# Another hand-written order for the loading phase of an attention and gated-FFN kernel on Trainium2

## Chip, core and metric

The kernel runs on one NeuronCore of a Trainium2 chip. PE is the matrix engine (its weight loads are PEld), DVE the vector engine, ACT the scalar engine, POOL is GpSimd, SP the engine that issues DMAs. Each engine works through its own queue in order; engines meet at semaphores. The metric is device time per execution in microseconds (us), as the median of several runs. The change is judged against 0.5%, about 1.13 us.

## What is computed

```python
# x (8, 8, 512, 64), state (8, 8, 32, 64): batch, head, row, depth
a  = softmax(x @ state^T / 8)        # each of 512 rows over 32 states
a2 = softmax(state @ x^T / 8)        # each of 32 states over 512 rows
y  = concatenate([a @ state, a2 @ x], axis=rows)   # per batch 512 + 32 rows
t  = heads of y side by side          # 8*544 = 4352 rows of 512
out = (sigmoid(t @ w_gate) * (t @ w_val)) @ w_out  # w: 512x1536, 1536x512
```

Both softmaxes come from one exponential of the scores. The kernel uses bfloat16 operands and float32 accumulation; the sigmoid is written as (tanh(z/2)+1)/2, its half folded into the last copy.

## The kernel before, in words

For one batch b the work runs as follows. `load_x` brings x in float32 (tile xf), `cast_x` makes bfloat16 of it (xb), two of eight heads at a time. x is transposed to xT, for batches 0 and 1 on PE into PSUM with a copy out (`xT_mm`, `xT_cp`, L101-L119), for the others by DMA transposes on SP's queue (`at_xT_dma`, L121). The state is loaded (`load_s`, `load_sb`), transposed on PE (`sT_mm`) and copied into sTc (`sT_cp`) or, zero-padded by head parity, into sTz (`sT_pad`, `pad`). `S_mm` makes the scores and `S_exp` their exponentials E on ACT. From E come Eb in bfloat16 (`at_Eb`, POOL), row sums and normalised weights ab (`n_sum`, `n_mul`, DVE), and aT, ab transposed (`aT_mm` and `aT_cp`, or `aT_dma`). Sums over rows for the second softmax are folded on POOL (`p_tok`, `p_fold`) or made on PE, and `sr_mm`, `sr_fin` give the 32 state rows.

The first product is regrouped: state @ w_gate and state @ w_val come first (`sw_visit`, `sw_wide`, L271-L302, into PSUM; `sw_cp`, L304, copies them to the tile SW), and `gv_mm(b, f, place)` multiplies SW by aT: two PSUM banks, gate and value, for the f-th 128 of 1536 columns, four matmuls of 512 columns. `gv_th` (tanh, ACT) reads the gate bank, `gv_glu` (DVE) the value bank, and glu is the left side of the second product, `out_mm(b, k)`: four matmuls each, three k for each quarter c of a batch's rows, then a copy on ACT and a store through SP.

PSUM has eight banks: two in the pool GV, one each in OU and AT, four in SWP. A call's `place` names the pool it takes a bank from; the bank is free once its last reader has run.

The order is written out by hand, one call after another, under `tc.manual_schedule()`: what is written first stands first in its engine's queue. L424-L673 are the prologue: batches 0 and 1 in full up to the product, the weights' loads, and batch 2 up to its aT. From L675 a loop over b = 2 to 8 pairs the second product of batch b-1 with the first product of b and prepares b+1; b = 8 stands for the state rows of all batches. The loop is the same before and after.

These parts of the prologue matter here:

- `warm(n, place)` (L381) issues n matmuls of 128 columns on the constant tile `ones`, whose results nobody reads. They keep PE busy ahead of its first real work.
- Weights are loaded with a cast on POOL's queue (`load_w(w, lo, n)` for columns lo to lo+n of w_gate (w=0) or w_val (w=1); `load_wo(q)` for a third of w_out). POOL also casts, folds and pads, and its DMAs stand in its queue between these.
- `pre` is a tile whose first column is filled by a first Exp (L438).
- `gate(landed)` (L80) is a POOL copy of one column of a tile, so that POOL's queue waits until that tile has landed. L594 puts one on batch 2's xT right ahead of load_wo(1); load_wo(2) follows it in the queue.
- For batch 2, cast_x(2) (POOL and DVE, L571 and L582) leads to at_xT_dma(2) (L590), S_mm(2) (L608, L610) and then n_sums, n_muls and aT_dma(2).

Of the kernel before, what the change touches and what calls it, by code (L numbers as in the profile page):

```python
# [16 lines left out]
def kernel(  # L17
# [70 lines left out]
    def cast_x(b, cp, lo, n):  # L88
        if b not in xbs:
            xbs[b] = xp.tile((128, 4, H, D), BF, name="xb")  # L90
        cp(xbs[b].rearrange("p c h d -> p h c d")[:, lo:lo + n], xfs[b][:, lo:lo + n])  # L91
# [289 lines left out]
    def warm(n, place):  # L381

        ps = place[0].tile((128, 512), FP, name="warm", tag=place[1])
        for _ in range(n):
            nc.tensor.matmul(ps[:, :128], ones[:, 0], ones[:, 0], start=True, stop=True)
# [39 lines left out]
    load_x(0, nc.sync, 4)
    load_x(1, nc.sync, 4)
    make_identity(nc, ident)
    for e in range(2):
# [1 line left out]
        nc.vector.memset(ones[:, e, 64 - e * 64:128 - e * 64], 0.0)  # L430
    nc.vector.memset(sTz, 0.0)
# [5 lines left out]
    pre = wp.tile((128, 2), FP, name="pre")
    nc.scalar.activation(pre[:, 0:1], ones[:, 0, 0:1], AF.Exp)  # L438

    cast_x(0, pool, 0, 2)  # L440
    load_w(1, 256, 256)
    load_w(0, 256, 256)
    load_sb(1)
    cast_s(0, vec)
    cast_x(0, pool, 4, 2)
    warm(20, SWP)
    load_w(0, 1024, 512)
    warm(16, OU)
    xT_mm(0, 0, OU)
    sT_mm(0, SWP)  # L450
    xT_cp(0, 0, vec)
    warm(20, OU)
    cast_x(0, act, 2, 2)
    cast_x(0, vec, 6, 2)
    xT_mm(0, 1, SWP)
    sT_pad(0, 0, vec)
    sT_pad(0, 1, act)
    S_mm(0, 0, SWP, (0,))
    xT_cp(0, 1, vec)
    xT_mm(0, 2, OU)  # L460
    cast_x(1, vec, 2, 2)
    cast_x(1, pool, 0, 2)
    xT_mm(0, 3, GV)
    load_w(1, 1024, 512)
    xT_cp(0, 2, act)
    cast_x(1, pool, 6, 2)
    xT_cp(0, 3, vec)
    cast_x(1, vec, 4, 2)
    load_w(0, 0, 256)
    load_sb(3)  # L470
    S_mm(0, 0, AT, (1,))
    S_exp(0, 0)
    S_mm(0, 1, AT, (0,))
    xT_mm2(1, 0, OU)
    S_mm(0, 1, OU, (1,))
    S_exp(0, 1)
    warm(12, AT)
    xT_cp2(1, 0, act)
    n_sum(0, 0)
    xT_mm2(1, 1, SWP)  # L480
    S_mm(1, 0, GV)
    n_sum(0, 1)
    xT_cp2(1, 1, vec)
    S_mm(1, 1, SWP)
    S_exp(1, 0)
    at_Eb(0)
    sw_visit(0, 256, 256)
    n_mul(0, 0, nc.vector)
    n_mul(0, 1, nc.vector)
    S_exp(1, 1)  # L490
    sT_mm(1, GV)
    sw_cp(0, 256, 2, 1, act)
    p_tok(1)
    n_sums(1)
    sw_cp(0, 256, 2, 0, act)
    aT_mm(0, GV)
    sT_cp(1, act)
    aT_cp(0, 0, act)
    sr_mm(0, AT)
    sw_visit(1, 256, 256)  # L500
    sw_visit(0, 1024, 512, 0)
    aT_cp(0, 1, vec)
    n_muls(1, nc.vector)
    load_sb(2)
    gv_mm(0, 3, GV)
    sw_cp(1, 256, 2, 0, act)
    sw_cp(1, 256, 2, 1, act)
    gv_th(0, 3)
    load_w(1, 0, 256)
    aT_mm(1, OU)  # L510
    sw_cp(0, 1024, 0, 1, act)
    sw_visit(1, 1024, 512, 0)
    sw_cp(0, 1024, 0, 0, vec)
    gv_glu(0, 3)
# [4 lines left out]
    sw_visit(1, 1024, 512, 1)
    sw_cp(0, 1024, 1, 1, vec)  # L520
    gv_mm(0, 11, GV)
    aT_cp(1, None, vec)
    sw_cp(1, 1024, 1, 0, act)
    gv_mm(0, 2, SWP)
# [8 lines left out]
    load_x(2, nc.gpsimd)
    gv_mm(0, 9, SWP)
    gv_glu(0, 11)
    gv_mm(1, 8, GV)
    gv_th(0, 9)
# [7 lines left out]
    gv_glu(1, 8)
    sw_cp(1, 0, 2, 1, act)
    gv_mm(0, 8, GV)
    sT_mm(2, AT)
    sw_cp(1, 0, 2, 0, act)
    sw_visit(0, 512, 512, 0)  # L550
    sw_cp(0, 0, 2, 0, vec)
# [6 lines left out]
    gv_mm(1, 11, GV)
    load_wo(0)
    sw_cp(0, 512, 0, 0, act)  # L560
    sw_cp(0, 512, 0, 1, vec)
    gv_th(1, 11)
    gv_mm(0, 0, SWP)
    gv_glu(1, 11)
    gv_mm(1, 9, GV)
    sw_cp(1, 512, 0, 1, act)
    at_Eb(1)
    sw_cp(1, 512, 0, 0, act)
    gv_th(1, 9)
# [9 lines left out]
    sr_mm(1, AT)
    gv_glu(0, 1)  # L580
    gate(xfs[0][:, 7, 0, 0:1])
    cast_x(2, pool, 0, 4)  # L582
    sw_visit(0, 512, 512, 1)
# [15 lines left out]
    sr_fin(1)
    gv_mm(0, 6, SWP)  # L600
    gv_mm(0, 7, GV)
    gv_mm(0, 4, SWP)
    gv_th(0, 6)
    gv_th(0, 7)
    out_mm(0, 1, OU)
# [1 line left out]
    gv_th(0, 4)
    S_mm(2, 1, SWP)  # L608
    gv_mm(1, 4, SWP)
    S_mm(2, 0, GV)  # L610
    gv_glu(0, 4)
    gv_glu(0, 7)
# [3 lines left out]
    gv_mm(1, 6, GV)
    gv_th(1, 4)
    gv_th(1, 6)
    out_mm(0, 0, AT)
    gv_glu(1, 6)  # L620
    gv_mm(1, 7, GV)
    gv_glu(1, 4)
# [4 lines left out]
    n_sums(2)
    load_x(3, nc.gpsimd)
    out_mm(0, 3)
    n_add(2)  # L630
# [1 line left out]
    n_muls(2, nc.vector)
    out_mm(0, 9)
    at_Eb(2)
    aT_dma(2)
# [1 line left out]
    out_mm(0, 4)
    gv_th(1, 3)
    gv_glu(1, 3)
    out_mm(0, 5)  # L640
    out_mm(0, 11)
    gv_mm(1, 1, GV)
    gv_th(1, 1)
    sw_wide(2, 0)
    out_mm(0, 6, GV)
# [4 lines left out]
    sw_cp(2, 0, 1, 1, act)  # L650
    sw_cp(2, 0, 2, 1, act)
    sw_cp(2, 0, 0, 0, vec)
    out_mm(0, 8)
    cast_x(3, pool, 0, 4)
    sw_cp(2, 0, 2, 0, act)
    sw_wide(2, 1)
    cast_x(3, act, 4, 4)
    sw_cp(2, 1, 1, 0, act)
    sw_cp(2, 1, 0, 0, act)
# [1 line left out]
    at_xT_dma(3)
    sw_cp(2, 1, 1, 1, vec)
    out_mm(0, 10)
    sw_cp(2, 1, 2, 1, vec)
    gv_mm(1, 10, SWP)
    sw_cp(2, 1, 0, 1, vec)
# [88 lines left out]
```

## Time and profile before

| what | value |
|---|---|
| time, median of 3 runs | 226.27 us (226.02 to 227.07) |
| span of the profiled execution, first to last instruction | 225.4 us |
| difference of the two | 0.87 us |
| first real PE work (a transpose of x) | 4.97 us |
| first gate/value matmuls, gv_mm(0, 3) | 16.20 us |
| wo thirds landed | 32.56, 44.09, 47.38 us |
| batch 2's xT: transposes issued, last landed | 29.95, 37.67 us |
| x(3) landed | 50.98 us |
| first sw_wide of the loop | 57.56 us |

Times inside the profile count from its first instruction. The timeline's rows read: start, duration, engine, line, operation, tile written <- tiles read, shape, number of instructions merged, and in brackets the idle time of the engine ahead of the row with what ended it. A row of several PE matmuls lasts from the start of its first to the end of its last, and the end of one lies well behind the start of the next.

### The profile page before, as it was taken

How to read it: one execution, taken by the hardware profiler on the slowest of the kernel's cores; microseconds unless marked ns; L12 is line 12 of the kernel's file. 1: busy time of each engine (PE TensorE's matmuls, PEld its weight loads, DVE VectorE, ACT ScalarE, POOL GpSimd, SP SyncE). 2: the span in 40 equal slices, each digit the busy share in tenths (PEclk: the TensorE clock that was granted, in tenths of full speed). 3: DMA queues.
4: the chain of work that ended last, by engine and by line, in shares of the span. 5: the costliest groups of instructions: out<-in, count | busy, mean ns of one | idle time of the engine just before them, and what ended most of it. 6: DMA issues, size and time to landing. Idle time of an engine off the chain costs nothing.

```text
span 225.4 us, 4817 instructions
## 1 busy us (share of the span) xinstructions
PE 216.1 (96%) x1843; PEld 110.5 (49%) x1843; DVE 132.2 (59%) x228; ACT 128.7 (57%) x242; POOL 77.6 (34%) x164
## 2 busy tenths in 40 slices
PE   7689999899999999999999999999999999999994
PEld 6654444334444444444444444444445444466744
DVE  3799997647658554855585638574766434422301
ACT  3468885339576566757574666656755444433311
POOL 4999832481027502660068005900370000000001
PEclk9999999999999999999999999999999999999999
DMA  6999992995496245614671441236112111111113
GB/s 208 276 204 193 287 157 48 138 261 167 92 292 223 47 93 165 210 35 86 153 245 26 86 126 47 69 70 143 47 61 81 48 47 49 72 69 49 47 33 108
DMA packets 38503, 27.38 MB, mean 121 GB/s; under 512 B 21104, under 2 KB 33776, under 8 KB 38480
## 3 DMA queue, kind: packets, MB, share of 16 engines
q1 hardware_dynamic: 31344, 19.74, 31.2%
q0 software_dynamic: 6848, 7.14, 17.1%
q8 instruction: 14, 0.23, 0.4%
q10 hardware_dynamic: 288, 0.20, 0.4%
q14 instruction: 9, 0.07, 0.1%
HBM read 18.35 MB, written 8.91 MB: 121 GB/s over the span
## 4 chain that ended last, share of the span: by engine, by line
PE 74%; DMA 12%; SPq 4%; POOL 4%; ACT 3%; issue 1%; DVE 1%; POOLq 0%
PE outp L351 34%; PE gvp L320 28%; DMA xf<-in_x_dram 6%; PE gvp L323 5%; SPq L124 4%; DMA wo<-in_moe_w_out_dram 4%; PE swp L268 3%; DMA xT<-xb 2%; PE Sp L132 2%; PE outp L371 1%; ACT SW L306 1%; PE srp L245 1%; POOL sTz L420 1%; SPq L74 1%; ACT E L137 1%
## 5 line engine op out<-in xcount | busy, mean ns | idle before, releaser
L335 DVE SCALAR_TENSOR_TENSOR glu<-th,gvp 128x512 bf16<-128x512 f32 (+1 forms) x108 | 70.0, 656 | 75.9 <-ACT th L330 61.8
L351 PE MATMUL outp<-wo,glu 128*128 128x512 bf16 x396 | 98.5, 379 | 1.2 <-DMA wo<-in_moe_w_out_dram 1.2
L320 PE MATMUL gvp<-aT,SW 128*128 128x512 bf16 x384 | 96.5, 379 | 0.0
L330 ACT ACTIVATE th<-gvp 128x512 f32<-128x512 f32 (+1 forms) x108 | 61.5, 574 | 59.2 <-PE gvp L320 47.1
L320 PEld LDWEIGHTS <-SW 128*128 128x128 bf16 x384 | 36.3, 98 | 45.1 <-issue 3.7
L351 PEld LDWEIGHTS <-glu 128*128 128x128 bf16 x396 | 37.4, 98 | 42.3 <-issue 2.2
L306 ACT CAST SW<-swp 128x512 bf16<-128x512 f32 x73 | 40.5, 588 | 3.9 <-PE swp L268 2.5
L143 POOL CAST Eb<-E 128x256 bf16<-128x256 f32 x32 | 12.0, 427 | 63.1 <-ACT E L137 63.1
L355 ACT ACTIVATE res<-outp 128x512 f32<-128x512 f32 x33 | 19.7, 597 | 19.6 <-PE outp L351 19.5
L362 POOL DMA_DIRECT2D out_dram<-res x2 | 1.1, 532 | 52.4 <-ACT res L355 52.4
L306 DVE CAST SW<-swp 128x512 bf16<-128x512 f32 x23 | 15.2, 681 | 0.0
L91 POOL CAST xb<-xf 128x1024 bf16<-128x1024 f32 (+1 forms) x14 | 12.8, 927 | 3.2 <-DMA xf<-in_x_dram 2.6
L137 ACT ACTIVATE E<-Sp 128x512 f32<-128x512 f32 x16 | 9.6, 602 | 3.4 <-PE Sp L132 3.4
L183 POOL COPY F<-G 32x128 f32<-32x128 f32 x28 | 9.9, 353 | 1.3
L204 DVE TENSOR_TENSOR ab<-E,ri 128x512 bf16<-128x512 f32 x12 | 8.7, 735 | 0.0
L268 PE MATMUL swp<-wg,sTc 64*32 64x512 bf16 (+1 forms) x192 | 8.6, 328 | 0.0
L132 PE MATMUL Sp<-sTz,xT 128*128 128x64 bf16 x128 | 7.0, 193 | 1.6 <-DVE xT L119 0.6
L132 PEld LDWEIGHTS <-xT 128*128 128x128 bf16 x128 | 6.0, 98 | 5.1 <-DVE xT L119 0.7
L178 POOL COPY F<-E 64x128 f32<-64x128 f32 x14 | 4.1, 292 | 12.3 <-DVE E L170 11.8
L150 DVE TENSOR_REDUCE rs<-E 128x16 f32<-128x512 f32 x12 | 8.2, 679 | 0.2 <-ACT E L137 0.2
L268 PEld LDWEIGHTS <-sTc 64*32 64x32 bf16 x384 | 4.5, 91 | 7.6 <-issue 5.4
L250 DVE RECIPROCAL r<-srp 128x128 f32<-128x128 f32 x8 | 7.6, 949 | 0.7 <-PE srp L245 0.7
(75 smaller groups left out, 150.3 us busy)
## 6 DMA issues: line engine op xcount, KB each, us to landing
out_dram<-res SPq DMA_DIRECT2D x31, 256.0 KB, 2.6
xf<-in_x_dram SPq DMA_DIRECT2D x4, 1024.0 KB, 6.3
xf<-in_x_dram SPq DMA_DIRECT2D x8, 256.0 KB, 4.5
xf<-in_x_dram POOLq DMA_DIRECT2D x2, 1024.0 KB, 10.1
wo<-in_moe_w_out_dram POOLq DMA_DIRECT2D x3, 512.0 KB, 8.3
wg<-in_moe_w_gate_dram POOLq DMA_DIRECT2D x2, 512.0 KB, 7.4
wv<-in_moe_w_val_dram POOLq DMA_DIRECT2D x2, 512.0 KB, 9.8
wv<-in_moe_w_val_dram POOLq DMA_DIRECT2D x2, 256.0 KB, 5.5
```

The costliest lines, as they stand in the source:

```text
L91: cp(xbs[b].rearrange("p c h d -> p h c d")[:, lo:lo + n], xfs[b][:, lo:lo + n])
L132: nc.tensor.matmul(ps[:, c, :, jj], xTs[b][:, 2 * i + jj, c], sTz[:, b, 2 * i + jj], start=True, stop=True)
L137: nc.scalar.activation(E1s[b][:, :, :, 2 * i:2 * i + 2].rearrange("p c e j n -> p (c e) j n"), held["S", b, i].rearrange("p c e j n -> p ( ...
L143: nc.gpsimd.tensor_copy(Ebs[b][:, c], E1s[b][:, c])
L268: nc.tensor.matmul(pss[e][j * Ns:(j + 1) * Ns, o:o + n], sTc[rows, b, j] if b > 1 else sTz[rows, b, j, e], (wg, wv)[w][rows, j, lo:lo + n] ...
L306: cp(*sw_left.pop((b, lo, w, e)))
L320: nc.tensor.matmul(ps, SWs[b][:, g, w, fs], aTs[b][:, :, g], start=(g == 0), stop=(g == 1))
L323: nc.tensor.matmul(ps, (wg, wv)[w][:, j, fs], XS[:, j], start=(j == 0), stop=(j == 3))
L330: nc.scalar.activation(th, held["gv", b, f][0], AF.Tanh, scale=0.5)
L335: nc.vector.scalar_tensor_tensor(glus[b][:, f], held["th", b, f], 1.0, held["gv", b, f][1], ALU.add, ALU.mult)
L351: nc.tensor.matmul(ops[b, c], glus[b][:, f, c * 128:(c + 1) * 128], wo[:, f], start=(f == 0), stop=(f == NF - 1))
L355: nc.scalar.activation(res, ops[b, c], AF.Copy, scale=0.5)
```

## The change

The calls from L424 to L673 are written in another order, with some other engines and PSUM pools; the loads, matmuls and counts of work are the same but for the warm matmuls (68 in four calls before, 68 in four calls after, with other sizes ahead of the first transposes). All of L424-L673 is replaced by the new list, of which this is the core (leading lines whole up to gv_mm(0, 3)):

```diff
+    load_x(0, nc.sync, 4)
+    load_s(0, nc.scalar)
+    make_identity(nc, ident)
+    load_x(1, nc.sync, 4)
+    nc.vector.memset(sTz, 0.0)
+    for e in range(2):
+        nc.vector.memset(ones[:, e, e * 64:e * 64 + 64], 1.0)
+        nc.vector.memset(ones[:, e, 64 - e * 64:128 - e * 64], 0.0)
+    cast_s(0, pool)
+    warm(20, GV)
+    load_w(0, 256, 256)
+    warm(20, GV)
+    cast_x(0, vec, 0, 2)
+    sT_mm(0, OU)
+    xT_mm(0, 0, GV)
+    load_w(1, 256, 256)
+    sT_pad(0, 1, act)
+    sT_pad(0, 0, vec)
+    xT_cp(0, 0, vec)
+    nc.scalar.activation(pre[:, 0:1], ones[:, 0, 0:1], AF.Exp)
+    warm(16, AT)
+    cast_x(0, pool, 2, 2)
+    cast_x(0, act, 4, 2)
+    cast_x(1, vec, 0, 2)
+    load_w(0, 1024, 512)
+    xT_mm(0, 1, SWP)
+    load_w(1, 1024, 512)
+    cast_x(0, act, 6, 2)
+    load_sb(2)
+    nc.gpsimd.memset(pick, 0.0)
+    xT_mm(0, 2, GV)
+    S_mm(0, 0, SWP, (0,))
+    xT_cp(0, 2, vec)
+    load_sb(1)
+    xT_cp(0, 1, act)
+    xT_mm(0, 3, SWP)
+    cast_x(1, vec, 2, 2)
+    S_mm(0, 0, OU, (1,))
+    S_mm(0, 1, AT, (0,))
+    xT_cp(0, 3, act)
+    S_mm(0, 1, AT, (1,))
+    cast_x(1, pool, 4, 2)
+    S_exp(0, 0)
+    cast_x(1, act, 6, 2)
+    load_w(0, 0, 256)
+    xT_mm2(1, 0, SWP)
+    n_sum(0, 0)
+    xT_mm2(1, 1, OU)
+    S_exp(0, 1)
+    at_Eb(0)
+    xT_cp2(1, 0, vec)
+    warm(12, GV)
+    S_mm(1, 0, GV)
+    xT_cp2(1, 1, act)
+    load_sb(3)
+    n_mul(0, 0, nc.vector)
+    S_mm(1, 1, OU)
+    n_sum(0, 1)
+    n_mul(0, 1, nc.vector)
+    load_w(1, 0, 256)
+    S_exp(1, 0)
+    sw_visit(0, 256, 256)
+    S_exp(1, 1)
+    sw_cp(0, 256, 2, 1, act)
+    sw_visit(1, 256, 256)
+    sr_mm(0, OU)
+    sw_cp(1, 256, 2, 1, act)
+    aT_mm(0, AT)
+    sw_visit(1, 1024, 512, 0)
+    load_w(0, 512, 512)
+    sw_cp(1, 256, 2, 0, act)
+    gate(xfs[0][:, 7, 0, 0:1])
+    n_sums(1)
+    sw_cp(0, 256, 2, 0, act)
+    aT_cp(0, 1, vec)
+    aT_cp(0, 0, act)
+    sw_visit(0, 1024, 512, 0)
+    n_muls(1, nc.vector)
+    gv_mm(0, 3, GV)
+    sw_cp(0, 1024, 0, 1, vec)
+    sw_cp(1, 1024, 0, 0, act)
+    gv_th(0, 3)
+    sw_cp(1, 1024, 0, 1, vec)
+    aT_mm(1, AT)
+    p_tok(1)
+    sw_cp(0, 1024, 0, 0, act)
+    sw_visit(1, 1024, 512, 1)
+    aT_cp(1, None, act)
+    gv_glu(0, 3)
+    sw_visit(0, 1024, 512, 1)
+    sw_cp(0, 1024, 1, 1, act)
...
+    at_Eb(1)
+    sw_cp(0, 1024, 1, 0, act)
+    sr_fin(0)
+    sw_cp(1, 1024, 1, 1, act)
+    gv_mm(0, 2, GV)
+    gv_mm(0, 11, SWP)
+    load_x(2, nc.gpsimd)
+    sw_cp(1, 1024, 1, 0, vec)
...
+    sT_mm(2, GV)
+    sT_mm(1, OU)
+    load_w(1, 512, 512)
...
+    sT_mm(3, AT)
+    sT_cp(2, vec)
...
+    load_wo(0)
...
+    p_fold(1)
...
+    gv_mm(1, 11, GV)
...
+    sT_cp(1, vec)
...
+    cast_x(2, pool, 0, 4)
+    load_wo(1)
...
+    cast_x(2, pool, 4, 4)
...
+    gv_mm(0, 5, SWP)
+    sw_cp(1, 512, 1, 1, vec)
+    sT_cp(3, act)
...
+    at_xT_dma(2)
...
+    out_mm(0, 1, AT)
+    pad(2, 6)
...
+    load_wo(2)
...
+    out_mm(0, 0, OU)
+    S_mm(2, 0, GV)
+    load_x(3, nc.gpsimd)
+    S_mm(2, 1, SWP)
...
+    gv_mm(1, 7, SWP)
+    n_sums(2)
+    n_muls(2, nc.vector)
+    n_add(2)
+    cast_x(3, vec, 4, 4)
+    gv_th(1, 7)
+    out_mm(0, 3)
+    out_mm(0, 2)
+    at_Eb(2)
+    gv_mm(1, 3, GV)
+    gate(xTs[2][:, 0, 3, 0:1])
+    gv_th(1, 3)
+    out_mm(0, 9)
+    gv_glu(1, 3)
+    cast_x(3, act, 0, 4)
+    aT_dma(2)
+    out_mm(0, 5)
+    gv_glu(1, 7)
+    out_mm(0, 11)
+    at_xT_dma(3)
+    out_mm(0, 4)
+    gv_mm(1, 1, GV)
+    sw_wide(2, 0)
...
+    gv_mm(1, 5, GV)
```

In the new order the gate on batch 2's xT stands alone, behind all weight loads, and no load follows it on POOL.

More of the change, by code (lines that the diff above doesn't have):

```diff
@@ L422 @@
     sbs = {}
+    load_x(0, nc.sync, 4)
+    ident_e = ident.rearrange("p (g e u) -> p e g u", e=2, u=8)
     load_s(0, nc.scalar)
-    load_x(0, nc.sync, 4)
+    make_identity(nc, ident)
     load_x(1, nc.sync, 4)
-    make_identity(nc, ident)
+    nc.vector.memset(sTz, 0.0)
+    pick = wp.tile((128, 128), BF, name="pick")
+    pre = wp.tile((128, 2), FP, name="pre")
     for e in range(2):
@@ L430 @@
         nc.vector.memset(ones[:, e, 64 - e * 64:128 - e * 64], 0.0)
-    nc.vector.memset(sTz, 0.0)
-    ident_e = ident.rearrange("p (g e u) -> p e g u", e=2, u=8)
-    pick = wp.tile((128, 128), BF, name="pick")
-    nc.gpsimd.memset(pick, 0.0)
+    cast_s(0, pool)
[10 more added lines that the diff above has]
+    nc.scalar.activation(pre[:, 0:1], ones[:, 0, 0:1], AF.Exp)
@@ L435 @@
+    sw_visit(1, 1024, 512, 1)
[3 more added lines that the diff above has]
+    sw_cp(0, 1024, 1, 1, act)
     for e in range(2):
         nc.gpsimd.memset(pick[e * 64:e * 64 + 64, e * 64:e * 64 + 64], 1.0)
[L437 to L514, printed above, removed]
@@ L515 @@
-    sw_cp(1, 1024, 0, 1, act)
-    sw_visit(0, 1024, 512, 1)
-    sw_cp(1, 1024, 0, 0, vec)
-    sw_cp(0, 1024, 1, 0, act)
[L519 to L524, printed above, removed]
+    at_Eb(1)
+    sw_cp(0, 1024, 1, 0, act)
+    sr_fin(0)
     sw_cp(1, 1024, 1, 1, act)
-    load_w(0, 512, 512)
+    gv_mm(0, 2, GV)
+    gv_mm(0, 11, SWP)
+    load_x(2, nc.gpsimd)
+    sw_cp(1, 1024, 1, 0, vec)
@@ L527 @@
     gv_th(0, 2)
+    gv_mm(0, 9, SWP)
     gv_th(0, 11)
-    gv_mm(1, 2, SWP)
-    sr_fin(0)
     gv_glu(0, 2)
+    gv_mm(1, 2, GV)
+    gv_glu(0, 11)
+    gv_th(0, 9)
     gv_th(1, 2)
[L533 to L537, printed above, removed]
+    gv_mm(1, 8, SWP)
+    sT_mm(2, GV)
+    sT_mm(1, OU)
+    load_w(1, 512, 512)
+    gv_glu(0, 9)
+    gv_glu(1, 2)
+    sT_mm(3, AT)
+    sT_cp(2, vec)
     gv_th(1, 8)
-    sT_mm(3, OU)
-    gv_glu(1, 2)
+    gv_glu(1, 8)
@@ L541 @@
     sw_visit(1, 0, 256)
-    gv_glu(0, 9)
-    load_w(1, 512, 512)
-    sw_visit(0, 0, 256)
[L545 to L551, printed above, removed]
+    sw_cp(1, 0, 2, 1, vec)
+    sw_cp(1, 0, 2, 0, act)
+    load_wo(0)
+    gv_mm(0, 8, GV)
+    sw_visit(0, 512, 512, 0)
+    sw_visit(0, 0, 256)
+    p_fold(1)
     gv_th(0, 8)
+    gv_glu(0, 8)
+    sw_cp(0, 0, 2, 0, act)
+    gv_mm(1, 11, GV)
@@ L553 @@
+    gv_th(1, 11)
     sw_cp(0, 0, 2, 1, vec)
-    sT_cp(2, act)
-    gv_glu(0, 8)
-    sT_cp(3, act)
-    sw_visit(1, 512, 512, 0)
[L558 to L569, printed above, removed]
+    gv_glu(1, 11)
+    gv_mm(1, 9, SWP)
+    sT_cp(1, vec)
+    sw_cp(0, 512, 0, 1, act)
+    gv_th(1, 9)
@@ L570 @@
+    sw_cp(0, 512, 0, 0, act)
+    gv_mm(0, 0, GV)
+    gv_glu(1, 9)
+    sw_visit(1, 512, 512, 0)
+    cast_x(2, pool, 0, 4)
+    load_wo(1)
     gv_th(0, 0)
-    cast_x(2, vec, 4, 4)
-    p_fold(1)
-    gv_glu(1, 9)
     gv_mm(0, 1, SWP)
-    gv_mm(0, 10, GV)
     gv_th(0, 1)
     gv_glu(0, 0)
-    gv_th(0, 10)
[L579 to L583, printed above, removed]
+    sw_cp(1, 512, 0, 1, vec)
+    gv_mm(0, 10, GV)
+    gv_glu(0, 1)
@@ L584 @@
+    sr_mm(1, OU)
+    sw_cp(1, 512, 0, 0, act)
+    cast_x(2, pool, 4, 4)
+    sw_visit(0, 512, 512, 1)
+    gv_th(0, 10)
     gv_glu(0, 10)
+    sw_cp(0, 512, 1, 0, act)
     sw_visit(1, 512, 512, 1)
-    sw_cp(0, 512, 1, 0, vec)
     sw_cp(0, 512, 1, 1, act)
     gv_mm(1, 0, GV)
-    pad(2, 6)
-    at_xT_dma(2)
+    gv_mm(0, 5, SWP)
     sw_cp(1, 512, 1, 1, vec)
-    sw_cp(1, 512, 1, 0, act)
-    gv_mm(0, 5, SWP)
-    gate(xTs[2][:, 0, 3, 0:1]); load_wo(1)
+    sT_cp(3, act)
+    sw_cp(1, 512, 1, 0, vec)
@@ L595 @@
     gv_th(1, 0)
+    gv_mm(0, 7, SWP)
+    gv_th(0, 7)
     gv_th(0, 5)
     gv_glu(1, 0)
-    gv_glu(0, 5)
[L599 to L605, printed above, removed]
-    gv_glu(0, 6)
[L607 to L612, printed above, removed]
+    at_xT_dma(2)
+    gv_mm(0, 4, GV)
+    sr_fin(1)
+    gv_th(0, 4)
+    out_mm(0, 1, AT)
+    pad(2, 6)
+    gv_glu(0, 7)
@@ L613 @@
+    gv_glu(0, 4)
+    gv_mm(0, 6, SWP)
+    gv_th(0, 6)
+    gv_mm(1, 6, SWP)
+    gv_mm(1, 4, GV)
+    gv_th(1, 6)
+    load_wo(2)
+    gv_glu(0, 5)
+    gv_th(1, 4)
+    out_mm(0, 0, OU)
+    S_mm(2, 0, GV)
+    load_x(3, nc.gpsimd)
+    S_mm(2, 1, SWP)
+    gv_glu(0, 6)
     out_mm(0, 7, SWP)
+    gv_glu(1, 6)
+    gv_glu(1, 4)
     S_exp(2, 1)
     S_exp(2, 0)
[L616 to L622, printed above, removed]
+    gv_mm(1, 7, SWP)
@@ L623 @@
+    n_sums(2)
+    n_muls(2, nc.vector)
+    n_add(2)
+    cast_x(3, vec, 4, 4)
     gv_th(1, 7)
-    gv_mm(1, 3, SWP)
-    load_wo(2)
+    out_mm(0, 3)
     out_mm(0, 2)
[L627 to L630, printed above, removed]
-    gv_glu(1, 7)
[L632 to L635, printed above, removed]
-    p_fold(2)
[L637 to L645, printed above, removed]
@@ L646 @@
-    gv_glu(1, 1)
-    sw_cp(2, 0, 0, 1, act)
-    sw_cp(2, 0, 1, 0, act)
-    sr_mm(2, GV)
[L650 to L659, printed above, removed]
-    sr_fin(2)
[L661 to L666, printed above, removed]
+    at_Eb(2)
@@ new lines @@
+    gv_mm(1, 3, GV)
[6 more added lines that the diff above has]
+    out_mm(0, 5)
+    gv_glu(1, 7)
+    out_mm(0, 11)
[3 more added lines that the diff above has]
+    sw_wide(2, 0)
+    gv_th(1, 1)
+    sw_cp(2, 0, 0, 1, vec)
+    load_x(4, nc.sync)
+    out_mm(0, 6, GV)
+    sw_cp(2, 0, 1, 1, act)
+    sw_cp(2, 0, 1, 0, vec)
+    out_mm(0, 8)
+    sw_cp(2, 0, 2, 0, act)
+    sw_cp(2, 0, 0, 0, vec)
+    sw_cp(2, 0, 2, 1, act)
@@ L667 @@
+    sw_wide(2, 1)
+    gv_glu(1, 1)
+    p_fold(2)
+    sw_cp(2, 1, 2, 1, act)
+    sr_mm(2, GV)
+    sw_cp(2, 1, 0, 0, vec)
+    sw_cp(2, 1, 1, 1, act)
+    sw_cp(2, 1, 0, 1, act)
+    out_mm(0, 10)
+    gv_mm(1, 10, SWP)
+    sw_cp(2, 1, 1, 0, vec)
+    sr_fin(2)
     gv_th(1, 10)
@@ L669 @@
     gv_mm(1, 5, GV)
+    gv_glu(1, 10)
     gv_th(1, 5)
-    gv_glu(1, 10)
-    load_x(4, nc.sync)
     gv_glu(1, 5)
```

## The prediction

> **What bounds the kernel now.** I read the busy table and the slices of the page first, then the chain of waits, then the timeline of single engines.
>
> ```profile
> PE 216.1 (96%) x1843; PEld 110.5 (49%) x1843; DVE 132.2 (59%) x228; ACT 128.7 (57%) x242; POOL 77.6 (34%) x164
> PE   7689999899999999999999999999999999999994
> POOL 4999832481027502660068005900370000000001
> DMA  6999992995496245614671441236112111111113
> ```
>
> TensorE is the bound from the fourth slice on. In the chain, batches 2 to 7 are PE pieces of 0.86 us end to end, and the loop repeats every 23.47 us (swp pieces at 69.88 and 93.35). The diff changes nothing there. So the change is worth what it does to the time at which the loop's first sw_wide starts (57.56), and the chain shows two places ahead of it: the start, and the output weights.
>
> ```profile
> 44.13 2.75 PE L351 MATMUL outp<-wo,glu 128*128 128x512 bf16 x12 [0.68 <-DMA wo<-in_moe_w_out_dram]
> 47.42 2.75 PE L351 MATMUL outp<-wo,glu 128*128 128x512 bf16 x12 [0.54 <-DMA wo<-in_moe_w_out_dram]
> ```
>
> A matmul of 512 columns lasts 379 ns, but the next starts 216 ns after it, so idle time of 0.68 is 0.84 lost and 0.54 is 0.70. Stepping from start to start in the same way, PE loses after its first gate/value group (16.20): 0.27 (aT of batch 1 waits for ab), 0.32 (wv), 0.71 (a bank), 0.31 (S_mm(2) waits for xT), 0.84 and 0.70 (wo): **3.15 us** in all. The rest is dense, so ahead of 16.20 and these 3.15 us are all there is to win.
>
> **The start, replayed.** I follow each engine's queue in the new order with the durations of these rows; consecutive ACT and DVE instructions overlap by about 0.07 (ACT: 13.15 to 13.64 for a 0.60 row).
>
> ```profile
> 1.04 3.47 PE L385 MATMUL warm<-ones 128*128 128x128 bf16 x36 [1.04 <-DVE ones L430]
> 1.21 1.28 ACT L438 ACT_TABLE_LOAD   x1 [1.21 <-PEq L739]
> 2.50 0.20 ACT L438 ACTIVATE pre<-ones 128x1 f32<-128x1 bf16 x1
> 4.92 0.62 ACT L91 CAST xb<-xf 128x512 bf16<-128x512 f32 x1 [2.22 <-DMA xf<-in_x_dram]
> 1.26 0.91 DVE L431 MEMSET sTz<- 128x1024 uint32 x1 [0.16 <-issue]
> 14.04 1.21 DVE L156 TENSOR_REDUCE rs<-E 128x32 f32<-128x1024 f32 x1
> 16.20 1.04 PE L320 MATMUL gvp<-aT,SW 128*128 128x512 bf16 x4
> ```
>
> DVE clears sTz (0.91) ahead of ones, so the warm matmuls start at 1.95, not 1.04, and there are 40, not 36. Before, starts were 107 ns apart until 3.74 (2.70 after the first) and 56 ns from there. With the same 2.70, 25 matmuls at 107 ns and 15 at 56 ns end at 5.5. The state's cast moves to POOL (landed 3.52, done by 4.0) and waits for nobody. sT_mm follows at 5.5 (before: 5.30), and sT_pad(0,1) is ACT's first computation: 5.97 to 6.33. Here is the costly edit: the Exp of `pre`, and with it the table load, which before sat in ACT's idle time at 1.21, now stands behind sT_pad: 1.28 + 0.20, until 7.8, while both x casts given to ACT wait. They end at 8.37 and 8.92; before, POOL and DVE had the same halves by 7.80. From here ACT is back to back: xT_cp(0,1) 9.44, xT_cp(0,3) 10.0, S_exp(0,0) 10.53, cast 11.08, S_exp(0,1) 11.6, xT_cp2 12.57, S_exp(1,0) 13.46 (a third of a us of waiting for DVE's xT_cp2, which n_sum(0,0) now precedes), S_exp(1,1) 14.0 (before 13.75), four evacuations 16.12 (before: two ahead of this point), aT_cp(0,0) 16.68. DVE reaches the other half of aT at 16.55, behind n_sums(1). So the first gate/value group starts at 16.7: **+0.5**. PE's other inputs are there: sr_mm(0) from 14.05, its Eb done at 13.55; the first 256 columns of the weights by 12.4 as before; wg's 512 at 15.4 (15.68 less some 0.3, since one 64 KB state load no longer lies ahead in POOL's queue).
>
> The work between that point and the loop changes little: sT_mm(1) now comes after it (+0.34), one more sw_visit comes before it (-0.25): **+0.1**.
>
> **Stalls after it.** Banks come free in the order in which their readers are written; I gave each bank to the next user in that order. aT_mm(1) waits 0.36 for n_muls(1) (ends 17.9); sw_visit(1,1024,·,1) 0.15 and sw_visit(0,1024,·,1) 0.35 for DVE's evacuations (18.5, 19.1); gv_mm(0,11) 0.5 for ACT's two evacuations of its own columns (20.8, behind the 1.0 us aT copy of batch 1, which ACT now has instead of DVE); gv_mm(1,11) 0.3 and gv_mm(0,5) 0.2 likewise. That makes 1.9. From 27 us on the other evacuations that change engine (sT_cp(1), sT_cp(2), one half of several visits) are done before their bank is wanted, with 0.2 to 1.5 us to spare; if that cover goes, each costs its row, 0.60 on ACT or 0.68 on DVE.
>
> The two wo stalls go. On POOL, load_wo(1) now follows cast_x(2, first half), so it is issued at 28.5 and lands behind the third of wo already in that queue: 32.56 + 2.9 = 35.4; out_mm(0,3) wants it at 43.4. load_wo(2) stands behind pad(2,6), which waits for sT_cp(3) (34.4 on ACT) and takes 2.06: issued 36.5, landing 5.8 later as the one at 38.25 did: 42.3, wanted at 46.8. The transposes of batch 2 start at 30.3 (before 29.95), now beside wo(1). Their last landed 7.7 us after the first issue: 38.0; S_mm(2) comes 2.6 us of PE work later than before, at 41.0, so its 0.31 goes too. x(3) is issued 37.2 and lands 3.6 behind wo(2), 45.9. DVE's cast of it is wanted free at 46.8. What is late next is therefore DVE: glu(1,3), behind that cast, ends at 48.7, and gv_mm(1,1) wants its bank at 49.4. On SP aT_dma(2) ends near 52.5 and batch 3's transposes follow at about 60 instead of 62.38, so the 0.31 that S_mm(3) lost at 62.1 goes as well: **-0.3**.
>
> Stalls: 1.9 - 3.15 = **-1.25**. The replay takes every hand-off as free of more than 0.05; rows show 0.02 (DMA to ACT) to 0.13 (DMA to POOL, 4.17 to 4.30). For the dozen bank hand-offs on which it stands I add 12 x 0.05 = **+0.6**.
>
> **The sum.** 0.5 + 0.1 - 1.25 - 0.3 + 0.6 = -0.35 us. The profiled span of 225.4 becomes 225.05; the median of the runs lies 0.87 above the span, so 226.27 - 0.35 = **225.9**. A change under 0.5% (1.13 us) is about what a measurement of this kernel can't tell from none.
>
> **Unknown costs.** No row shows a table load with ACT work ahead of it. From below it costs nothing (if it runs at the head of the queue as before): then the x landings and wg bound the start, the first group comes at 15.9, and the sum is -1.15. From above I take twice the row, 2.56, so +1.28. I take the row itself, 1.28, since the `pre` that follows it in the trace starts 0.01 after it. [...]
>
> **Rivals.**
>
> 1. *ACT becomes the bound of the loading stage* (slower). From 6.0 to 16.7 ACT has 18 instructions in a chain with one gap of 0.33. Each us added anywhere in it moves the first group by the same. If they don't overlap (18 x 0.07 = 1.3), or the load costs its upper end (1.28), the sum is +0.95, so 227.2, and both give 228.5. It decides once the chain is over 0.35 longer than I count. For it: evacuations follow each other with both PE and DVE feeding them. Against it: before, ACT rows do overlap wherever their input was ready. Chance 0.30.
>
> 2. *PE's fast clock opens later.* Only one start of the fast spacing is in the trace, 2.70 after the first warm matmul; nothing shows that it follows the first matmul and not a time of its own. If it opens after all 40, these take 40 x 0.107 = 4.28 and end at 6.23, and sT_mm ends 0.2 later still: ACT's chain starts 0.9 later, nothing absorbs it, and the sum is +0.55, so 226.8. Before, 36 at 107 ns would have ended at 4.9, just as x came, so that order was covered. [...] Chance 0.18.
>
> 3. *The start is not longer*, because the table load isn't where I put it or ACT's waits are shorter: -1.15 as above, 225.1, and 224.8 if the hand-offs cost nothing too. For it: x and the weights land as before. Chance 0.15.
>
> 4. *The output weights collide with the transposes*, so that taking the hold away gains nothing. The aT transpose issued at 46.89 beside x(3) landed after 4.4 us, later ones after 2.4. Two us on the last of batch 2's is hidden (38.0 against 41.0); if all waited until wo(2) and x(3) had passed (44 to 46), S_mm(2) would lose 3 to 5 us: 229 to 231. Chance 0.05.
>
> My forecast has 0.32. The range 224.8 to 228.2 leaves out the tail of rivals 1 and 4 and a start better than all bounds: about 2 in 10. Faster by over 0.5% (under 225.14) takes most of rival 3 and the lower edge of the forecast: 0.22. Slower (over 227.4) takes half of rival 1, rival 4 and what the replay may have missed behind 20 us: 0.30. The rest, 0.48, is no change that counts.
>
> **What would show it.** Right: ACT_TABLE_LOAD near 6.3 with x casts behind it; the first L320 matmul near 16.7; no wo wait on an L351 row; S_mm(2) and S_mm(3) without a wait for xT; the loop's first sw_wide near 57.2. Wrong: a table load at 1.2; the first L320 before 16 or after 17.7; PE idle between 40 and 50 us for xT or for a glu behind the cast of x(3); warm matmuls that end after 6.

## The result, and the profile after

The changed kernel takes 235.8 us (median of 4 runs, 234.06 to 237.98), the kernel before 226.15 (4 runs, 225.73 to 227.07). The ratio is **1.039** (95% interval 1.0349 to 1.0431): 3.9% slower, far outside the predicted 224.8 to 228.2. The profiled run of after is its slowest (237.98, mean granted clock 0.978 against 0.984 or 0.985) and is left out of the ratio; the other three have a median of 235.05 and spans of 232.3 to 234.8, so about 2 us of what follows may be that run's own.

The order of reading is that of the prediction. First the page of after: busy table and slices.

```profile
PE 219.3 (93%) x1843; PEld 111.6 (47%) x1843; DVE 132.1 (56%) x228; ACT 129.8 (55%) x243; POOL 76.5 (32%) x163
PE   6989997059999999999999999999999999999994
PEclk9999999758999999999999999999999999999999
```

A slice is 5.9 us here. PE, 9 in nearly every slice before, falls to 7, 0 and 5 in the slices from 35 to 53 us, and the granted clock to 7, 5 and 8 in those from 41 to 59 us. The loop behind has the old rhythm. PE's waits, longest first (in all, times, longest), name the cause:

```profile
PE Sp L132 <- DMA xT<-xb: 9.7, 3, 5.2
```

and PE's timeline shows the place, first before, where S_mm(2) hardly waits, then after:

```profile
37.31 0.25 PE L132 MATMUL Sp<-sTz,xT 128*128 128x64 bf16 x3
37.72 0.32 PE L132 MATMUL Sp<-sTz,xT 128*128 128x64 bf16 x5 [0.16 <-DMA xT<-xb]
```

```profile
38.86 1.03 PE L351 MATMUL outp<-wo,glu 128*128 128x512 bf16 x4
39.72 0.19 PE L132 MATMUL Sp<-sTz,xT 128*128 128x64 bf16 x1
42.14 0.20 PE L132 MATMUL Sp<-sTz,xT 128*128 128x64 bf16 x1 [2.22 <-DMA xT<-xb]
44.56 0.20 PE L132 MATMUL Sp<-sTz,xT 128*128 128x64 bf16 x1 [2.22 <-DMA xT<-xb]
49.99 0.88 PE L132 MATMUL Sp<-sTz,xT 128*128 128x64 bf16 x13 [5.23 <-DMA xT<-xb]
50.68 1.89 PE L351 MATMUL outp<-wo,glu 128*128 128x512 bf16 x4
```

S_mm(2, 0) takes one matmul for each of batch 2's four transposes as it lands, and loses 2.37 + 2.38 + 5.39 = **10.1 us** from start to start. The last row lasts 1.89 us for four matmuls that took 1.03 at 38.86: half rate. The idle time ahead of these rows is the loss; a second price is that PE comes back slow. The windows table gives start and end, time, PE, PEld, DVE, ACT and POOL busy (instructions), clock, DMA share (packet times summed over 16 engines, which can pass 1) and GB/s:

```profile
32.00:38.00 6.00, 6.00 (x33) 2.70 (x30) 5.47 (x10) 4.12 (x9) 3.23 (x4) 1.00 1.34 126
38.00:44.00 6.00, 2.12 (x11) 0.87 (x9) 1.76 (x3) 0.96 (x2) 0.00 (x0) 1.00 1.39 114
44.00:50.00 6.00, 0.21 (x2) 0.11 (x2) 0.00 (x0) 0.00 (x0) 0.00 (x0) 0.56 0.72 210
50.00:56.00 6.00, 6.00 (x28) 2.71 (x29) 3.81 (x6) 1.68 (x3) 1.56 (x5) 0.58 0.01 3
```

The clock's own records put it at half from 44.74 to 54.98, 10.24 us. Ten matmuls of 512 columns start 427 ns apart in it instead of 216: 2.1 us.

The transposes explain the wait. Their rows on SP's queue, first before, then after (ns of the issue, then us from issue to landing, each shortest, median and longest):

```profile
L124 SPq DMA_TRANSPOSE xT<-xb x4: 1264/1354/1760, 29.9 to 34.6; - x4
DMA to landing us min/median/max: 2.5/2.9/4.0
```

```profile
L124 SPq DMA_TRANSPOSE xT<-xb x4: 1286/1781/2076, 31.1 to 36.1; - x4
DMA to landing us min/median/max: 8.5/9.5/13.8
```

In after they landed at 39.65, 42.09, 44.52 and 49.95. The other queue was loading meanwhile: wo thirds issued at 29.25 and 34.92 (landed 39.48, 47.84), x(3) at 35.65 (landed 50.80). The loop's first sw_wide starts at 68.13 instead of 57.56, +10.6. The two wo waits and S_mm(3)'s did go.

### The profile page after: what moved, and what is told of

It is laid out like the page before. It is cut to its first block, busy times and chain, and to the rows that moved or that the text cites. A ratio compares the mean times of both kernels' runs of the same rounds, so it can differ in the third digit from the quotient of the medians.

```text
span 236.2 us, 4820 instructions
## 1 busy us (share of the span) xinstructions
PE 219.3 (93%) x1843; PEld 111.6 (47%) x1843; DVE 132.1 (56%) x228; ACT 129.8 (55%) x243; POOL 76.5 (32%) x163
## 4 chain that ended last, share of the span: by engine, by line
PE 77%; DMA 12%; POOL 5%; SPq 3%; issue 1%; ACT 0%; DVE 0%; POOLq 0%
PE outp L351 36%; PE gvp L320 29%; DMA xT<-xb 6%; DMA xf<-in_x_dram 6%; PE gvp L323 4%; PE swp L268 4%; SPq L124 2%; PE Sp L132 1%; POOL Eb L143 1%; SPq L74 1%; PE srp L245 1%; PE outp L371 1%; POOL P L197 1%; POOL xb L91 1%; POOL wo L85 0%
## 5 line engine op out<-in xcount | busy, mean ns | idle before, releaser
L351 PE MATMUL outp<-wo,glu 128*128 128x512 bf16 x396 | 99.7, 383 | 0.0
L320 PE MATMUL gvp<-aT,SW 128*128 128x512 bf16 x384 | 97.9, 382 | 0.2
L351 PEld LDWEIGHTS <-glu 128*128 128x128 bf16 x396 | 37.9, 99 | 41.7 <-issue 1.9
L306 ACT CAST SW<-swp 128x512 bf16<-128x512 f32 x72 | 40.0, 586 | 5.1 <-PE swp L268 3.9
L306 DVE CAST SW<-swp 128x512 bf16<-128x512 f32 x24 | 16.0, 684 | 3.5 <-PE swp L268 3.2
L132 PE MATMUL Sp<-sTz,xT 128*128 128x64 bf16 x128 | 7.4, 198 | 10.1 <-DMA xT<-xb 9.7
L91 POOL CAST xb<-xf 128x1024 bf16<-128x1024 f32 (+1 forms) x12 | 11.5, 974 | 0.8 <-DMA xf<-in_x_dram 0.5
L156 DVE TENSOR_REDUCE rs<-E 128x32 f32<-128x1024 f32 x2 | 2.4, 1214 | 12.1 <-ACT E L137 12.1
L385 PE MATMUL warm<-ones 128*128 128x128 bf16 x68 | 6.3, 275 | 2.1 <-DVE ones L434 2.1
L178 POOL COPY F<-E 64x128 f32<-64x128 f32 x14 | 4.4, 313 | 12.1 <-DVE E L170 11.6
```

The lines of the kernel that those rows point to most:

```text
L132: nc.tensor.matmul(ps[:, c, :, jj], xTs[b][:, 2 * i + jj, c], sTz[:, b, 2 * i + jj], start=True, stop=True)
L306: cp(*sw_left.pop((b, lo, w, e)))
L320: nc.tensor.matmul(ps, SWs[b][:, g, w, fs], aTs[b][:, :, g], start=(g == 0), stop=(g == 1))
L351: nc.tensor.matmul(ops[b, c], glus[b][:, f, c * 128:(c + 1) * 128], wo[:, f], start=(f == 0), stop=(f == NF - 1))
```

## The experiments

The theory after this result: batch 2's transposes and POOL's loads slow each other, and the hold before existed for that. Rivals: the new order of S_mm(2) and its neighbours is slow by itself, or only the cast or only x(3) harms. Each diff is against the kernel named.

**Hold the loads again** (against after; wo(1), wo(2) and x(3) behind a gate on batch 2's xT):

```diff
-    load_wo(1)                         # behind cast_x(2, pool, 0, 4)
+    gate(xTs[2][:, 0, 3, 0:1])        # right ahead of load_wo(2)
+    load_wo(1)
-    gate(xTs[2][:, 0, 3, 0:1])         # behind gv_mm(1, 3, GV)
```

> The new order with the hold put back: the gate on batch 2's xT, then load_wo(1), load_wo(2) and load_x(3) behind it on POOL. Theory A (loads in flight beside the transposes slow both): the transposes land 8 us after their first issue, near 39, S_mm(2) waits less than 0.5 us, PE stays at 216 ns per matmul, the second and third parts of wo cost 1 to 3 us of waiting on out_mm; 225 to 228 us. Rival B (something else of the new order makes the transposes late: both casts of x(2) on POOL, the pads, PE's order): S_mm(2) still waits about 10 us; 233 us or more.

232.63 us, ratio 1.0279 (1.025 to 1.0307). The transposes are as quick as before again (6.7 us from first issue to last landing), and S_mm(2) waits for nothing:

```profile
40.12 0.63 PE L132 MATMUL Sp<-sTz,xT 128*128 128x64 bf16 x16
40.59 1.03 PE L351 MATMUL outp<-wo,glu 128*128 128x512 bf16 x4
44.38 1.67 PE L351 MATMUL outp<-wo,glu 128*128 128x512 bf16 x7 [1.90 <-DMA wo<-in_moe_w_out_dram]
53.16 0.59 PE L320 MATMUL gvp<-aT,SW 128*128 128x512 bf16 x2 [2.15 <-DVE glu L335]
```

But the time did not come back to 226, and the 225 to 228 expected is missed. The new order wants wo(1) 2.06 us before it is there (landed 44.34), and a glu stands behind DVE's cast of x(3), which now lands at 51.73; that costs 2.3. The clock's records then show half rate from 54.07 to 57.48, and the stretch from sw_wide(2, 0) to sw_wide(2, 1) takes 4.09 us (54.32 to 58.41) where the new order with PE's transposes, below, takes 2.60. So the transposes' part is as the theory had it; what the hold costs in the new order I had too low.

**Take only the gate away** (against before, L594):

```diff
-    gate(xTs[2][:, 0, 3, 0:1]); load_wo(1)
+    load_wo(1)
```

> The kernel before with one edit: the gate ahead of load_wo(1) taken out, so that load_wo(1), load_wo(2) and load_x(3) are issued from 30.5 us on, while the four transposes of batch 2 run. Theory A: the last transpose lands 10 us or more later than 37.7, S_mm(2) waits 8 to 12 us, some matmuls then run at half rate; 233 to 239 us. Rival B: the two waits for wo go and nothing comes in their place; 224.5 to 225.5 us.

235.47 us, ratio **1.0398** (1.0365 to 1.0431). This one line gives a loss of the same size, in the old order:

```profile
37.88 0.19 PE L132 MATMUL Sp<-sTz,xT 128*128 128x64 bf16 x1
42.95 0.23 PE L132 MATMUL Sp<-sTz,xT 128*128 128x64 bf16 x1 [4.88 <-DMA xT<-xb]
46.05 0.23 PE L132 MATMUL Sp<-sTz,xT 128*128 128x64 bf16 x1 [2.86 <-DMA xT<-xb]
```

S_mm(2) loses 8.45 us here.

**Only x(3) beside the transposes** (against after; as the first, with `load_x(3)`, a plain copy of 1 MB without a cast, moved to the place behind cast_x(2, pool, 4, 4)):

> The new order with both later parts of wo held behind the transposes, but load_x(3), which moves 1 MB without a change of type, issued beside them. A1 (any load on POOL's queue collides): the last transpose lands after 42 and S_mm(2) waits 3 us or more; 229 us or more. A2 (only the loads that change float32 to bfloat16 collide): the transposes land by 40; 225 to 228 us.

235.45 us, ratio 1.0405 (1.0339 to 1.0471). The transposes landed at 40.77 to 42.44, all behind x(3) (39.77). A load without a cast collided as well: 10.90 us from first issue to last landing, against 6.70 with the hold. S_mm(2) loses only 1.9, not the 3 expected, since it comes late; the larger loss is out_mm's, 4.55 us for wo(1), which stood behind the late transposes (issued 43.37, landed 49.11). So it is the landings, not the time, that show the collision here:

```profile
42.09 0.20 PE L132 MATMUL Sp<-sTz,xT 128*128 128x64 bf16 x1 [0.86 <-DMA xT<-xb]
49.15 3.06 PE L351 MATMUL outp<-wo,glu 128*128 128x512 bf16 x7 [4.38 <-DMA wo<-in_moe_w_out_dram]
```

**Only wo(1) beside them** (against after; the gate ahead of load_wo(2), load_wo(1) left where it is):

> The new order with load_wo(2) and load_x(3) held, but load_wo(1) issued as in the new order, ahead of the second half of the cast of x(2). Theory A, if the delay grows with the bytes in flight: the first three transposes land as late as in the new order (39.6, 42.1, 44.5) and the last near 45 instead of 50, so S_mm(2) waits 5 us and PE does not fall to half rate for as long; 229 to 232 us. If one 512 KB load were harmless: the transposes land by 40 and the time is 225 to 228 us.

230.96 us as the median of four; ratio 1.018 (1.0129 to 1.0231), from three of them (229.21 to 231.34). The fourth, 233.49, is the one profiled. The last transpose landed at 41.73, 9.5 us after the first issue instead of 6.7. S_mm(2) did not wait, against the 5 us expected: in this profile PE ran at half rate from 11.89 to 15.30, its first gate/value group came at 18.74 and S_mm(2) at 42.08. A glu behind the cast of x(3) cost 2.85. The time lies in the range of theory A, but not by the wait that was to make it; what this run shows is the delay of the transposes.

**No transposes at all** (against before: batch 2's x transposed on PE, which has nothing on the DMA engines; 16 matmuls more, no gate, the loads as in the run without it):

```diff
-    at_xT_dma(2)
+    xT_mm2(2, 0, OU)   # and xT_mm2(2, 1, OU) after gv_mm(0, 6), each with xT_cp2 on ACT
-    gate(xTs[2][:, 0, 3, 0:1]); load_wo(1)
+    load_wo(1)
```

> The kernel before with batch 2's xT made by 16 transposes on PE (xT_mm2, xT_cp2) in place of the four DMA transposes, and the gate taken out, so that the later parts of wo and x(3) are loaded with nothing beside them that waits. Theory A: wo lands by 36 and 39, x(3) by 42; the waits for wo (0.84, 0.70) and for xT (0.31) go, PE gains 0.95 us of transposes; 225.0 to 226.0 us. Rival B (the loads are late for another reason, or the new copies on ACT hold up the banks): waits of 1 us or more on out_mm or S_mm remain; 227 us or more.

227.4 us, ratio 1.0045 (1.0029 to 1.0062). The same three loads now land at 36.72, 40.01 and 42.97 (beside the transposes 38.55, 42.40 and 45.59), and PE waits for none of them. The time is above the 225.0 to 226.0 expected.

**The same in the new order** (against after: the same 16 matmuls in AT, no gate, out_mm(0, 1) moved behind gv_mm(0, 6)):

> The new order with batch 2's xT made on PE in the same way and no gate, the loads of wo as early as the new order has them. Theory A (the whole loss comes from the transposes beside the loads): S_mm(2) waits for nothing, PE never falls to half rate after the start, and with the start (+0.3), the stalls of 3.15 us before that become about 1.5, and 0.95 us of transposes the time is 225.0 to 227.0 us. Rival B (the rest of the new order costs as well): 229 us or more.

227.73 us, ratio **1.0069** (1.0048 to 1.009). The place that lost 10 us is dense, and the clock never falls (1.00 in every window from 16 to 62 us):

```profile
40.65 1.03 PE L351 MATMUL outp<-wo,glu 128*128 128x512 bf16 x4
41.51 0.63 PE L132 MATMUL Sp<-sTz,xT 128*128 128x64 bf16 x16
41.98 1.03 PE L351 MATMUL outp<-wo,glu 128*128 128x512 bf16 x4
```

So once the collision is out, the new order and the old one differ by 0.24% or 0.5 us (0.33 by the medians), within the two intervals, of the 8.9 that the change cost (235.05 against 226.15). This time too is above its range (225.0 to 227.0). What these two lose against before (1.1 and 1.5 us by their medians) is in part the 16 matmuls (16 x 56 ns = 0.9). In the profiled runs 0.6 to 0.7 lies behind the last matmul (3.92 and 4.01 us from its start to the end, against 3.30 before); the next run has 3.91 there with DMA transposes, so that is not a price of PE's transposes.

**Keep PE busy in the gap** (against after; 40, 40 and 90 warm matmuls, which nobody reads, behind the first three matmuls of S_mm(2, 0)):

> The new order with 170 warm matmuls between the first four matmuls of S_mm(2, 0), which fill PE's waiting for the four transposes. If the ten matmuls of 427 ns that follow the wait come from PE having been idle, they go back to 216 ns and the time is 2.1 us below that of the new order: 233 to 234 us. If they come from something else (heat, the loads), the ten stay and the time is that of the new order, 234 to 237 us. In both cases the waits for the transposes themselves stay at about 10 us.

235.49 us, ratio 1.0418 (1.0378 to 1.0458); the clock record stays at full speed (1.00 from 44 to 56 us, where after has 0.56 and 0.58):

```profile
49.76 0.54 PE L132 MATMUL Sp<-sTz,xT 128*128 128x64 bf16 x13
50.13 1.03 PE L353 MATMUL outp<-wo,glu 128*128 128x512 bf16 x3
58.86 0.41 PE L270 MATMUL swp<-wg,sTc 64*32 64x512 bf16 x8
```

From the out_mm behind S_mm(2) to sw_wide(2, 0) it is 8.73 us (50.13 to 58.86) where after has 10.85 (50.68 to 61.53): the 2.1 us of half rate come from PE's idling. The total did not fall: the last transpose had landed at 45.95 in this run, and 90 matmuls were too many by 3.8 us. The forecast of time (233 to 234) missed, and by time alone the rival fits (234 to 237); the clock's records and the spacing decide for the mechanism. The same three loads stood beside the transposes as in after, yet here the last landed 14.86 us after the first issue (31.09 to 45.95), not 18.84.

**Cast x(3) earlier as well** (against before: the PE transposes above, with cast_x(3) and at_xT_dma(3) moved forward):

> The kernel before with batch 2's xT made on PE and no gate, as in the run with 16 transposes, and with x(3), which now lands at 43, cast some 5 us earlier, so that batch 3's DMA transposes run earlier too. If the 0.57 us that S_mm(3) still waited were what kept that version behind the kernel before: the wait goes and the time is 226.3 to 227.0 us. If the transposes on PE and the later start of the first gate/value group are the reason: the wait goes and the time stays within 0.3 us of 227.4.

227.2 us, ratio 1.0047 (1.0031 to 1.0063). The wait of S_mm(3) is gone from the trace (0.57 before this edit), the ratio did not move (1.0045 to 1.0047; the median fell 0.2, that of before beside it 0.13). That wait was not what kept it behind.

**wo in halves behind the gate** (against before: load_wo(1) and load_wo(2) as two DMAs of 256 KB each):

> The kernel before, hold kept, with the second and third parts of wo each loaded in two halves behind the gate. If PE's two waits for wo end with the landing of the whole part: the first matmuls of out_mm(0, 2) and out_mm(0, 4) start on the first half, about half of the 1.54 us goes and the time is 225.4 to 226.0 us. If the extra issues on POOL (0.6 us each) move the landings back by as much: 226 to 227 us.

226.44 us, ratio 1.0017 (0.9998 to 1.0036). Nothing gained, as the second expectation had it (226 to 227): the last half lands at 48.68, the whole part before at 47.38, and one wait of 0.71 for wo is left. The two wo waits that the prediction wanted to win are thus hard to win from this side too.

**The kernel before, again**, to see how much one profile of it varies:

> The kernel before once more, unchanged, for a second profile of it: how far its first gate/value group (16.20), its two waits for wo (0.84 and 0.70) and the opening of PE's clock (3.78 us) differ from one execution to another. Span 224.4 to 225.5 us. If the clock opens at a time of its own, it opens at another time than 3.78 us.

226.85 us, span 225.1; PE's full clock opened at 4.00 instead of 3.78. Its first gate/value matmul is at 16.87 (16.20 in the first profile), its waits for wo come to 0.5 us on PE instead of 1.54, S_mm(3) loses 0.63 instead of 0.31. The numbers of the prediction's 3.15 us of stalls vary from run to run by more than the 0.35 us of gain it reckoned with.

**How much does a load beside the transposes cost?** The runs so far had suggested that the two queues' times simply add. To try it (against before; wo(1) and wo(2) beside, x(3) behind the gate):

```diff
-    gate(xTs[2][:, 0, 3, 0:1]); load_wo(1)
+    load_wo(1)
-    load_x(3, nc.gpsimd)
+    gate(xTs[2][:, 0, 3, 0:1]); load_x(3, nc.gpsimd)
```

> Kernel before, with the two thirds of w_out issued beside batch 2's transposes as in the run without the gate, but x(3) held behind the gate. Theory A (the two queues share the engines, and their times add): the transposes take 6.7 us from first issue to last landing with nothing beside them (run with the hold), a third of w_out 3.3 us when the queue is full, so the last transpose lands 6.7 + 2 x 3.3 = 13.3 us after the first issue, 12.3 to 14.3; with x(3) (3.0 more) it was 16.0. S_mm(2) then loses 5 to 6.5 us, the two waits for w_out (1.5) go, and half-rate matmuls add 0 to 2.5: 229.5 to 233. Theory B (a load beside the transposes breaks them up, however much it moves): 16 us again, 8.4 lost and 235. Theory C (the loss comes from x(3) alone): under 10 us, and 225 to 228.

The last transpose landed at 43.17, **13.33 us** after the first issue (29.84): theory A's 13.3. S_mm(2) lost 5.28, as it had it:

```profile
37.82 0.19 PE L132 MATMUL Sp<-sTz,xT 128*128 128x64 bf16 x1
40.40 0.23 PE L132 MATMUL Sp<-sTz,xT 128*128 128x64 bf16 x1 [2.39 <-DMA xT<-xb]
42.86 0.81 PE L132 MATMUL Sp<-sTz,xT 128*128 128x64 bf16 x6 [2.23 <-DMA xT<-xb]
```

The time, 233.2 (ratio 1.0304, 1.0241 to 1.0367), is 0.2 above its range; half rate (40.39 to 47.21 by the clock's records) took 2.2 us of the 4.35 of work behind 42.86, and the wo waits it counted as won were only 0.5 in the second profile of before. All runs with these transposes beside each other:

| beside the transposes | first issue to last landing, us | over 6.70 | loads' own time, at 3.3 and 3.0 |
|---|---|---|---|
| nothing | 6.70 (6.5 and 7.7 in two profiles of before) | 0 | 0 |
| wo(1) | 9.52 | 2.8 | 3.3 |
| x(3) | 10.90 | 4.2 | 3.0 |
| wo(1), wo(2) | 13.33 | 6.6 | 6.6 |
| wo(1), wo(2), x(3), old order | 15.99 | 9.3 | 9.6 |
| wo(1), wo(2), x(3), new order with PE's gap filled | 14.86 | 8.2 | 9.6 |
| wo(1), wo(2), x(3), after | 18.84 | 12.1 | 9.6 |

The loads' own time is the spacing of landings where no transposes ran beside them (36.72 to 40.01 to 42.97). "Nothing" means none of these three loads: in every row the first third of wo still lands 1.8 to 3.2 us after the first issue (32.56 to 34.39). All rows but the last agree within 1.4 us; after is 2.5 over, in the profile of its 237.98 run. The last two rows have the same company in the same order, so a single profile can be off by some us: the sum is a rule that fits, not a law.

## Why the prediction was wrong, point by point

**The failed step** is "The transposes of batch 2 start at 30.3 (before 29.95), now beside wo(1). Their last landed 7.7 us after the first issue: 38.0; S_mm(2) comes 2.6 us of PE work later than before, at 41.0, so its 0.31 goes too." The start was 31.11 and S_mm(2) came at 39.72, near enough; the 7.7 us was taken from a trace in which the gate had kept the queue empty beside the transposes. With loads beside them it was 18.84, and PE stood idle between 40 and 50 us for xT, which the prediction had named as a sign of being wrong. That the loads slow them was shown by taking only the gate away (+4.0%) and by taking the transposes off the DMA engines (+0.7%). Rival 4 named this mechanism and priced it at 3 to 5 us, with 0.05; two errors made it so small. It took "until wo(2) and x(3) had passed" at landings of 44 to 46 that assumed loads at full speed, when they are slowed as well (47.84, 50.80); and it left out the half clock, 2.1 us. Adding the three loads' own times, which the trace of before showed (47.38 - 44.09 = 3.3 for a third of w_out, 50.98 - 47.38 = 3.6 for x(3)), to 7.7 gives 17.9 after the first issue: 48.2 from the prediction's 30.3, and 7.2 lost at 41.0. The durations were there; the sum was not made. That the times add was not known from that trace, though, and the filled gap's 14.86 shows how far one run can lie from it.

**The two wo stalls** went as forecast (-1.54 in that profile), and so did S_mm(3)'s 0.31. They are the gain, and the price, 10.14 + 2.1, is more than six times as large; in the second profile of before they cost only 0.5.

**The start** came out nearly as forecast in this profile, 16.45 for the first gate/value group against 16.7, by two errors that nearly cancel. The table load was not behind sT_pad:

```profile
2.02 1.28 ACT L414 ACT_TABLE_LOAD   x1 [2.02 <-DVE ones L434]
6.96 0.37 ACT L414 CAST sTz<-stp 64x256 bf16<-64x256 f32 x1 [3.66 <-PE stp L406]
7.35 0.20 ACT L446 ACTIVATE pre<-ones 128x1 f32<-128x1 bf16 x1
```

It carries the line of sT_pad's cast and ran in ACT's idle time ahead of it, and `pre` then took its 0.20 alone: rival 3's placement, 1.28 saved. What a load costs with ACT work ahead of it is not shown: in before nothing ran ahead of it (`pre` follows 0.01 behind it), and here it has idle time on both sides. Against that, the fast clock opened late, at 7.19 (3.78 in before), as rival 2 had it:

```profile
2.11 4.45 PE L385 MATMUL warm<-ones 128*128 128x128 bf16 x40 [2.11 <-DVE ones L434]
6.49 0.43 PE L406 MATMUL stp<-ident,sb 128*64 128x64 bf16 x8
```

Nearly all 40 went at 107 ns, and sT_mm came at 6.49, not 5.5; ACT was through with `pre` at 7.55 instead of 7.8. What ended last ahead of the group was then not ACT but wg's 512 columns, which the prediction had at 15.4:

```profile
15.77 0.62 PE L268 MATMUL swp<-wg,sTz 64*32 64x512 bf16 x16 [0.70 <-DMA wg<-in_moe_w_gate_dram]
16.45 1.02 PE L320 MATMUL gvp<-aT,SW 128*128 128x512 bf16 x4
```

So rival 1 (ACT as the bound of the start) did not decide in this profile. In three others with the same start it did: with the hold, with x(3) beside and with the gap filled, PE waits 0.32 for ACT's copy of aT, and the group comes at 17.12 to 17.19. Over the six profiles with the new start it came at 16.45 to 18.74 (median 17.14), over the seven with the old one at 16.20 to 17.93 (16.70): +0.4, close to the +0.5 of the forecast.

**Stalls after the first group** were forecast at 1.9 us, in six waits, five of them for banks. After shows one such wait, gv_mm's at 20.83 (0.30), and 0.49 for wv at 17.73: 0.8 us up to S_mm(2). The sum had banks too dear by about a us, which the collision hid. The pair of runs with PE's transposes bounds this part together with the start: old and new order are 0.5 us apart.

**The offset.** I put the median 0.87 above the span. Every later run has 1.75 to 1.8 between its own time and span, and 227.07 is 1.67 above the span of before: its profile was, as it seems, that of the 227.07 run, not of the median. This cost nothing in a difference. One bound of the range does not come out of its terms: rival 3 with hand-offs free is 225.1 - 0.6 = 224.5, not 224.8.

## What to carry to other kernels

A hold in front of a transfer may be protecting another transfer, not delaying its own (here its removal alone cost 4.0%): before removing it, add the durations of everything that will then be in flight together, and compare that sum, not each transfer's duration alone, with the moment at which PE wants the last of them. Here the sum came within 2.5 us in all profiles. A latency read from a trace held only for the company it had there (7.7 us in before, 18.84 in after). And a stretch of PE waits is to be charged with the half rate behind it (2.1 us in after, 1.5 with the hold, 2.2 beside two loads), also where no single gap is long (1.44 us at most in the run with wo in halves).
